# Gated sum of full and sliding-window attention: the sliding branch's weights read with a step of 20, not copied into padded columns

## The chip, the cores and the metric

The kernel runs on one core of a Trainium2 chip. A core has TensorE (matrix products, PE in the profile, with its weight loads as PEld), VectorE (DVE), ScalarE (ACT), GpSimd (POOL) and SyncE (SP, which here only issues DMA transfers), each with its own queue of instructions. The metric is the device time of one execution in microseconds, as the median over the runs.

## What is computed

Two attention branches read the same input x of 2,048 tokens by 640 features, each with its own weights. Both have 32 heads of 20 channels. A gate per token mixes them:

```python
g = _sigmoid((x * gate_w).sum(-1, keepdims=True))
a = _A_ref(x, A_wqkv, A_wo)
b = _B_ref(x, B_wqkv, B_wo)
return g * a + (1 - g) * b
```

Branch A is full softmax attention: `scores = q @ k.T * 20**-0.5` over all 2,048 keys, softmax, times v, then the output projection `wo`. Branch B, the sliding branch, lets each token see eight keys, at distances 0, 2, ... 14 behind it:

```python
off = jnp.arange(W) * dil          # W = 8, dil = 2
idx = pos[:, None] - off[None, :]
mask = idx >= 0
...
logits = jnp.einsum("bhsd,bhswd->bhsw", q, kg) * scale
logits = jnp.where(mask[None, None, :, :], logits, -1e9)
attn = _softmax(logits, axis=-1)
o = jnp.einsum("bhsw,bhswd->bhsd", attn, vg)
```

## The kernel before

**Branch A, the main loop.** The work on scores is cut into 32 groups (a block of 512 queries times four heads), and each group into 64 units (128 keys by 512 queries of one head). The main loop at the end of `_build` takes two or three units as a tile: `qk` (line 1610) writes their scores to PSUM, `exp` (line 1634) lets ScalarE compute the exponentials of the whole tile, and `pv` (line 1679) multiplies them by the values into `obank`. There are 704 tiles. When three units don't fit or the planner chooses so, a further unit "rides" on a tile: VectorE computes its exponential by integer arithmetic on the bits of the number (line 1624 writes `uD`), and three shifted copies of it (line 860 writes `eD`) are weighted and summed by further matmuls against scaled values `vS`, which GpSimd prepares (line 852). A ride thus moves work from ScalarE to VectorE and TensorE.

**Side work.** Between the tiles TensorE runs everything else on three PSUM banks (`side`): A's key, query and value projections (`gen_kd`, `gen_qd`, `gen_v`), the normalisation (`gen_norm`), the output projection (`gen_fold`), the gate, and all of branch B. The helper `mm_group` (line 605) issues these as matmuls in four column groups of 32 output rows; all of them stand at line 620 in the profile. Each has a weight load (LDWEIGHTS) of 128 rows by 32 columns.

**Branch B.** It goes in eight blocks of 256 tokens (`TOK`). `gen_bproj(u)` projects q, k and v of a block: 3 x 5 chunks of 128 output rows, each summed over 5 chunks of features, so 75 steps of four matmuls of 256 columns. VectorE casts the results to `qkvB` (line 919), and SP's queue copies v, shifted, to `vR` (line 927). `gen_b(u)` multiplies q by the shifted k on VectorE (line 945), sums over channels by matmuls with a selection matrix (line 955), takes the maximum and the exponential, multiplies by the shifted v (line 1042), sums (line 1052), and scales (line 1075). Channels are arranged so that chunk f holds channels f, 5 + f, 10 + f and 15 + f of all 32 heads: row 32 j + h of chunk f is channel 5 j + f of head h. Dense weights have that column at 20 h + 5 j + f, so the 32 columns of one weight load lie 20 elements apart.

**How B's weights come into that order.** One transfer (line 1440) brings B's q, k and v weights, dense, into the buffer `stage`. `gen_bweights` (line 869) then copies them on GpSimd in 15 pieces of 128 x 640 (line 878) into the buffer `kvw`, in the padded order, over A's weights: v's part (m = 2) goes over the padded key weights of A's first heads, q's part (m = 0) over A's key weights once A's key projection is done, and k's part (m = 1) over A's value weights once A's last value projection is done. The first `gen_bproj` waits for all of them (`done["bw"]`). `stage` is later used for the products of q and k and for `vR`.

**What sets the order.** Nothing is ordered at run time but by semaphores. A planner in Python (`_Sched`, and `step`, `order`, `run_side`, `next_tile`, `wanted` in `_build`) keeps a modelled clock for each engine, gives each instruction a modelled duration, and from that decides which generator goes next, whether a tile gets two or three units, and whether a unit rides. It has knobs: slack, priorities and idle thresholds. The table `PLAN` (line 50) gives all 18 knobs anew at certain tile numbers; it is the layout table of the change. Where TensorE would idle too long, the planner inserts filler matmuls (line 1700).

Of the kernel before, what the change touches and what calls it, by code (L numbers as in the profile page):

```python
# [6 lines left out]
BF16 = mybir.dt.bfloat16  # L7
# [7 lines left out]
P = 128  # L15
S = 2048
D = 640
H = 32
DH = 20
# [358 lines left out]
def _build(ctx, nc, A_x, A_wqkv, A_wo, B_wqkv, B_wo, gate_w, out):  # L378
# [20 lines left out]
    xT = sb([P, CN, S], BF16, "xT")  # L399
    WqP = sb([P, CN, P], BF16, "WqP")  # L400
    woA_z = _ap(WqP, 0, [[1, D]])
    kvw = sb([P, 3 * CN * D], BF16, "kvw")
    woA_d = sb([P, CN, D], BF16, "woA_d")
    woBp = sb([P, CN, D], BF16, "woBp")
    kT = sb([P, NQ, S], BF16, "kT")
# [1469 lines left out]
```

## Time and profile before

| what | value |
|---|---|
| median of three runs | 815.27 us (813.67 to 817.51) |
| profiled execution, its own time | 818.97 us |
| span of its instructions | 816.4 us |
| granted TensorE clock, mean | 0.991 |
| ScalarE busy | 782.7 us, 96% |
| TensorE busy | 753.3 us, 92% |
| VectorE busy | 718.1 us, 88% |
| GpSimd busy | 149.6 us, 18% |
| weight copies on GpSimd (line 878) | 15, 22.1 us, the first at 72.6 us and the last at 177.8 us |

In a group row, the columns after the bar are busy time in us and mean duration of one instruction in ns, then the idle time of the engine just before them and what ended it; `out<-in` names the buffers. In a timeline row, the first two numbers are start and duration in us, `xN` is the number of instructions merged into the row, and the bracket is the idle time before it. In a window row, each engine has its busy time in us and its count of instructions; PEclk is the clock that TensorE was granted, 1.00 being full speed. Busy times of TensorE are modelled at their ends: matmuls follow each other at a smaller distance than the duration of one.

### The profile page before, as it was taken

To read this page: it belongs to the slowest core of one execution; us is meant where nothing else is said; L and a number is where in the kernel's file an instruction comes from. 1 tells how busy PE (TensorE), PEld (TensorE's weight loads), DVE (VectorE), ACT (ScalarE), POOL (GpSimd) and SP (SyncE) were. 2 spreads that over 40 slices of the span, in tenths; PEclk is the share of its full clock that TensorE was granted. 3 is DMA by queue.
4 is the path that set the end of the run, shared out by engine and by line. 5 is a ranking of instruction groups with operands and counts; after the bars stand their busy time and mean duration, and the time that the engine had idled before them with its cause. 6 is when DMAs were issued, how large, how long until landed. Compare 5 with 4: busy or idle time off the path is not lost.

```text
span 816.4 us, 28733 instructions
## 1 busy us (share of the span) xinstructions
PE 753.3 (92%) x12136; PEld 276.9 (34%) x12138; DVE 718.1 (88%) x1228; ACT 782.7 (96%) x736; POOL 149.6 (18%) x207
## 2 busy tenths in 40 slices
PE   8999999989989999999898988989899999899987
PEld 5332222323333332333333332332243333333324
DVE  7588988579999999989999999898999899988964
ACT  4999999999999999999999999999999999999994
POOL 6014111351112111121112111121101221110110
PEclk9999999999999999999999999999999999999999
DMA  9112212201012231100121000303100130030210
GB/s 313 38 26 47 47 25 43 71 5 29 14 31 52 50 71 27 35 20 6 38 57 38 18 26 19 67 19 77 29 17 14 48 66 14 7 71 28 58 46 35
DMA packets 61458, 35.50 MB, mean 43 GB/s; under 512 B 27220, under 2 KB 60132, under 8 KB 61332
## 3 DMA queue, kind: packets, MB, share of 16 engines
q1 hardware_dynamic: 61044, 33.36, 16.7%
q8 instruction: 96, 1.57, 0.8%
q10 hardware_dynamic: 288, 0.33, 0.1%
q14 instruction: 30, 0.25, 0.1%
HBM read 12.00 MB, written 2.62 MB: 18 GB/s over the span
## 4 chain that ended last, share of the span: by engine, by line
DVE 30%; PE 26%; ACT 25%; issue 12%; SPq 5%; DMA 1%; POOL 0%; POOLq 0%; ACTq 0%; DVEq 0%
ACT ebuf L1634 24%; DVE uD L1624 11%; DVE eD L860 8%; PE score L1610 7%; PE obank L1679 7%; PE side L620 7%; DVE stage L945 3%; SPq L927 3%; PE score L620 2%; SPq L767 2%; DVE stage L1042 2%; DVE qkvB L919 1%; DVE oTt L821 1%; DMA stage<-qkvB 1%; PE score L1325 1%
## 5 line engine op out<-in xcount | busy, mean ns | idle before, releaser
L1634 ACT ACTIVATE ebuf<-score 128x1024 bf16<-128x1024 f32 (+1 forms) x704 | 770.8, 1252 | 13.7 <-PE score L1610 11.9
L1610 PE MATMUL score<-qT,kT 32*128 32x512 bf16 x2048 | 279.4, 386 | 36.0 <-ACT ebuf L1634 20.2
L1624 DVE TENSOR_SCALAR uD<-score 128x512 int16<-128x512 f32 x371 | 244.7, 680 | 24.3 <-PE score L1610 23.6
L860 DVE TENSOR_SCALAR eD<-uD 128x2048 int16<-128x2048 int16 (+1 forms) x279 | 194.8, 719 | 2.3 <-PE obank L1679 1.5
L1679 PE MATMUL obank<-ebuf,vA 128*21 128x512 bf16 x1677 | 156.6, 389 | 4.6 <-ACT ebuf L1634 1.6
L1610 PEld LDWEIGHTS score<-qT,kT 32*128 32x128 bf16 x2048 | 69.6, 91 | 266.0 <-ACT ebuf L1634 178.3
L852 POOL TENSOR_TENSOR vS<-vA,vw 128x252 bf16<-128x252 bf16 x93 | 69.1, 745 | 298.2 <-PE obank L1679 246.6
L620 PE MATMUL side<-xT,kvw 128*32 128x256 bf16 (+2 forms) x2720 | 118.1, 287 | 4.9 <-DVE qkvB L919 2.5
L1679 PE MATMUL obank<-eD,vS 128*21 128x512 bf16 x1113 | 99.2, 384 | 0.0
L620 PEld LDWEIGHTS side<-xT,kvw 128*32 128x32 bf16 (+1 forms) x2720 | 62.0, 96 | 49.9 <-issue 19.6
L1679 PEld LDWEIGHTS obank<-ebuf,vA 128*21 128x21 bf16 x1677 | 36.8, 89 | 87.5 <-issue 56.6
L827 POOL TENSOR_TENSOR rcp<-rcp,gA 128x16 f32<-128x16 f32 x31 | 9.0, 291 | 288.8 <-DVE rcp L825 288.8
L1042 DVE TENSOR_TENSOR stage<-stage,eB 128x2048 bf16<-128x2048 bf16 x40 | 49.7, 1255 | 1.0 <-DMA stage<-qkvB 1.0
L945 DVE TENSOR_TENSOR stage<-qkvB 128x2048 bf16<-128x2048 bf16 x40 | 49.6, 1263 | 0.1
L919 DVE CAST qkvB<-side 128x512 bf16<-128x512 f32 (+1 forms) x72 | 42.0, 592 | 4.3 <-PE side L620 4.1
L1679 PE MATMUL obank<-uD,vA 128*21 128x512 bf16 x371 | 36.9, 388 | 0.0
L1679 PEld LDWEIGHTS obank<-eD,vS 128*21 128x21 bf16 x1113 | 27.7, 92 | 18.8 <-issue 2.6
L833 POOL TENSOR_TENSOR oN<-oTt,rcp 128x512 bf16<-128x512 f32 x31 | 32.6, 1053 | 2.4
L620 PE MATMUL side<-woBp,oB 128*32 128x512 bf16 (+1 forms) x500 | 25.4, 304 | 1.3 <-DVE dst L724 0.5
L821 DVE STREAM_TRANSPOSE oTt<-obank 128x512 f32<-128x512 f32 x32 | 22.7, 708 | 4.5 <-PE obank L1679 4.4
L620 PE MATMUL side<-woA_d,oTd 128*32 128x512 bf16 (+1 forms) x496 | 25.7, 303 | 0.0
L620 PE MATMUL side<-xT,WqP 128*32 128x512 bf16 x320 | 24.3, 385 | 0.6 <-DVE qkvB L657 0.3
(170 smaller groups left out, 519.3 us busy)
## 6 DMA issues: line engine op xcount, KB each, us to landing
stage<-qkvB SPq DMA_DIRECT2D x128, 80.6 KB
WqP<-in_A_wqkv_dram SPq DMA_DIRECT2D x16, 160.0 KB
stage<-in_B_wqkv_dram SPq DMA_DIRECT2D x1, 2400.0 KB
oTd<-oN SPq DMA_DIRECT2D x108, 20.0 KB
qT<-dst SPq DMA_DIRECT2D x104, 20.0 KB
out_dram<-outsb SPq DMA_DIRECT2D x12, 160.0 KB
kvw<-in_A_wqkv_dram SPq DMA_DIRECT2D x2, 800.0 KB
oTd<-in_A_x_dram SPq DMA_DIRECT2D x2, 640.0 KB
```

Of the source, the lines that this page charges most:

```text
L620: ins = e.matmul(o[j:k, :], l(j) if callable(l) else l[:, j:k], r, start=(first and i == 0), stop=(last and i == n - 1), skip_group_check= ...
L821: T("dve", 0.625, lambda e: e.transpose(oTt[:, :], obank[:, :]), reads=["obank"], writes=["oTt"])
L833: T(en, c2, lambda e: e.tensor_tensor(oo, ii, ib, ALU.mult), reads=["rcp", "oTt"], writes=["oN0"])
L852: T("pool", 0.607, lambda e: e.tensor_tensor(vS[:, d % 2, :, :], _ap(vA, (kb * NQ + q) * 4 * DV, [[0, K - 1], [1, 4 * DV]]), _ap(vw, 0, [[ ...
L860: T("dve", 0.065 + 0.1334 * n, lambda e, k=k, sl=sl: e.tensor_scalar(eD[:, sl % NS, 0:512 * n].bitcast(I16), uD[d % 2][:, 0:512 * n].bitca ...
L919: t = TB(dvc(n * TOK), lambda e, o=o, i=i: e.tensor_copy(o, i), reads=[("side", b)], writes=[key])
L945: TB(dvc(CH, 2), lambda e: e.tensor_tensor(o, i0, i1, ALU.mult), reads=["qB", "kB"], writes=[("prod", i)] + (["stage"] if u == 0 else []), ...
L1042: TB(dvc(CH, 2), lambda e: e.tensor_tensor(o, i0, i1, ALU.mult), reads=["eB"] + [("vR", w4) for w4 in range(4)], writes=[("prod", i)], por ...
L1610: ins = e.matmul(o, kT[32 * j:32 * j + 32, q, kb * P:(kb + 1) * P], qT[g % NQT][32 * j:32 * j + 32, :], start=True, stop=True)
L1624: t = T("dve", 0.598, lambda e: e.tensor_scalar(uD[d % 2][:, 512 * i:512 * (i + 1)].bitcast(I16), side[x], UOFF, 0.0, op0=ALU.add, op1=ALU ...
L1634: exps[s] = T("act", actc(512 * n), lambda e: e.activation(ebuf[s % NE][:, 0:512 * n], score[s % 2][:, 0:512 * n], ACTF.Exp, scale=LN2 / S ...
L1679: ins = e.matmul(obank[32 * j:32 * j + DV, :], v, src, start=(kb == 0), stop=(last and k >= len(lst) - 4), skip_group_check=True)
```

## The change

The padded copies are gone. B's dense weights are loaded into a buffer of their own, `wBs`, and stay there for all eight blocks. The weight loads of `gen_bproj` read them in place: 32 columns with a step of 20 elements. The matmuls and their number stay as they are. The space is found by giving `stage` (products and `vR`) the same memory as `kvw`: it is written only when A's projections of k and v no longer need `kvw`. So `gen_bproj(0)` now waits for the end of the key projection instead of the copies, and before its shifted copies of v, and before the first products in `gen_b`, for A's last value projection. `gen_bweights` and its call are removed. The fourth block of x is staged in `wBs` instead of `stage`. The modelled duration of the projection's matmuls is the same as before.

`PLAN` has other rows: 101 changed ones in place of 99.

```diff
 PLAN = {
-    0: ((0.29, 0.69), 0.16, 1.0, 5.5, 0.94, -1.37, 0.17, 9.99, 7.0, 7.54, 0.6, 0.62, 5.69, 5.04, 0.0, 0.65, 2, -3),
...
+    0: ((0.29, 0.69), 0.16, 1.0, 5.5, 0.94, -1.37, 0.17, 9.99, 5.5, 6.98, 0.6, 0.62, 5.69, 5.04, 0.0, 0.62, 2, -1.5),
...
-    kvw = sb([P, 3 * CN * D], BF16, "kvw")
+    CH = WIN * TOK
+    NCH = 3
+    VW = TOK + DIL
+    kvw = sb([P, max(3 * CN * D, NCH * CH + 4 * CN * VW)], BF16, "kvw")
+    stage = kvw
...
-    stage = sb([P, NCH * CH + 4 * CN * VW], BF16, "stage")
+    wBs = sb([P, 3 * D * CN], BF16, "wBs")
...
-    XOFF = [(oTd, 0), (oTd, 4 * D), (oB, 0), (stage, 2 * D * CN)]
+    XOFF = [(oTd, 0), (oTd, 4 * D), (oB, 0), (wBs, 2 * D * CN)]
...
-    def gen_bweights():
-        for m in (2, 0, 1):
...
-                o = _ap(kvw, (m * CN + c) * D, [[P, CN], [32, 4], [1, 32]])
-                i = _ap(stage, c * 3 * D + m * D, [[1, CN], [CN, 4], [DH, 32]])
-                T("pool", 1.352, lambda e, o=o, i=i: e.tensor_copy(o, i), reads=["stage"],
-                  writes=[("WkA", "WvA", ("WkP", 0))[m], ("wBp", m)])
-        done["bw"] = True
...
     def gen_bproj(u):
         t0 = u * TOK
-        while not (done.get("bw") and (u == 0 or done.get(("bl", u - 1)))):
+        while not (done.get(("kd", CN - 1)) and (u == 0 or done.get(("bl", u - 1)))):
             yield ("cond",)
...
-                        kvw[:, (mm_ * CN + c) * D + f * P:(mm_ * CN + c) * D + (f + 1) * P],
+                        lambda j, mm_=mm_, c=c, f=f: _ap(wBs, c * 3 * D + mm_ * D + CN * (j // 32) + f, [[DH, 32]]),
                         xT[:, c, t0:t0 + TOK]) for c in range(CN)]
-                yield from mm_group(b, mms, [("wBp", mm_)] + XT(t0 // 512), mmc(TOK), first=True, per=2)
+                yield from mm_group(b, mms, ["wBs"] + XT(t0 // 512), mmc(TOK), first=True, per=2)
...
-        while u > 0 and not done.get(("bp", u - 1)):
+        while not (done.get(("bp", u - 1)) if u else done.get(("v", KBN - 1, 1))):
...
-              reads=["vB"], writes=[("vR", w4)] + (["stage"] if u == 0 else []), dma=True, nd=4, iss=0.65)
+              reads=["vB"], writes=[("vR", w4)] + (["WkA", "WvA", ("WkP", 0)] if u == 0 else []), dma=True, nd=4, iss=0.65)
...
     def gen_b(u):
-        while not (done.get(("bqk", u)) and (u == 0 or done.get(("bs", u - 1)))):
+        while not (done.get(("bqk", u)) and done.get(("v", KBN - 1, 1)) and (u == 0 or done.get(("bs", u - 1)))):
...
-               reads=["qB", "kB"], writes=[("prod", i)] + (["stage"] if u == 0 else []), port=True)
+               reads=["qB", "kB"], writes=[("prod", i)] + (["WkA", "WvA", ("WkP", 0)] if u == 0 else []), port=True)
...
-    T("sp", 10.0, lambda e: e.dma_start(_ap(stage, 0, [[3 * D, CN], [1, 3 * D]]), wB_v[:, :, :]), writes=["stage", ("xs", 3)], dma=True, iss=2.0)
+    T("sp", 10.0, lambda e: e.dma_start(_ap(wBs, 0, [[3 * D, CN], [1, 3 * D]]), wB_v[:, :, :]), writes=["wBs", ("xs", 3)], dma=True, iss=2.0)
...
-                if g1 == 2:
-                    add_gen(gen_bweights(), 4)
```

More of the change, by code (lines that the diff above doesn't have):

```diff
@@ L443, in _build @@
     vB = _ap(qkvB, CN * TOK + CN * (TOK + PADB), [[TOK + PADB, CN], [1, TOK + PADB]])
-    CH = WIN * TOK
-    NCH = 3
-    VW = TOK + DIL
-    stage = sb([P, NCH * CH + 4 * CN * VW], BF16, "stage")
+    wBs = sb([P, 3 * D * CN], BF16, "wBs")
     vR = _ap(stage, NCH * CH, [[VW, 4 * CN], [1, VW]])
@@ L867, in gen_d @@
         ulock[d % 2] = False
-    def gen_bweights():
-        for m in (2, 0, 1):
-            while m == 0 and not done.get(("kd", CN - 1)) or m == 1 and not done.get(("v", KBN - 1, 1)):
-                yield ("cond",)
-            for c in range(CN):
-                while sch.avail["pool"] > max(sch.avail["pe"], clock[0]):
-                    yield ("cond",)
-                o = _ap(kvw, (m * CN + c) * D, [[P, CN], [32, 4], [1, 32]])
-                i = _ap(stage, c * 3 * D + m * D, [[1, CN], [CN, 4], [DH, 32]])
-                T("pool", 1.352, lambda e, o=o, i=i: e.tensor_copy(o, i), reads=["stage"],
-                  writes=[("WkA", "WvA", ("WkP", 0))[m], ("wBp", m)])
-        done["bw"] = True
     bdone = [0.0]
```

198 rows, old and new, of the table PLAN are left out of this document.

## The prediction

> **What bounds the kernel now.** I read four views in this order: the page, the windows (busy time of each engine by stage), the groups of instructions by shape, and the timeline of single stretches.
>
> ```profile
> span 816.4 us, 28733 instructions
> ...
> PE 753.3 (92%) x12136; PEld 276.9 (34%) x12138; DVE 718.1 (88%) x1228; ACT 782.7 (96%) x736; POOL 149.6 (18%) x207
> ...
> DVE 30%; PE 26%; ACT 25%; issue 12%; SPq 5%; DMA 1%; POOL 0%; POOLq 0%; ACTq 0%; DVEq 0%
> ```
>
> The page names ScalarE: 96% busy. The chain that ended last passes through VectorE, TensorE and ScalarE about equally, and GpSimd (POOL) has 0% of it. So the 22 us of copies that the change removes are worth nothing as GpSimd time; they count only by what they do to others.
>
> ```profile
> core 0: us, PE busy (x) PEld busy (x) DVE busy (x) ACT busy (x) POOL busy (x), PEclk, DMA share, GB/s
> ...
> 140.00:168.00 28.00, 27.18 (x452) 10.37 (x450) 16.82 (x32) 27.00 (x27) 8.54 (x8) 1.00 0.23 57
> 168.00:187.00 19.00, 16.74 (x193) 4.43 (x195) 16.37 (x25) 17.43 (x18) 11.81 (x10) 0.91 0.05 10
> 187.00:300.00 113.00, 106.37 (x1819) 40.73 (x1819) 108.87 (x177) 111.94 (x104) 18.45 (x27) 1.00 0.17 40
> 300.00:500.00 200.00, 184.40 (x3007) 64.71 (x3004) 187.74 (x324) 198.09 (x192) 35.73 (x52) 1.00 0.12 29
> 500.00:700.00 200.00, 183.81 (x3065) 68.14 (x3062) 185.96 (x304) 199.28 (x186) 31.75 (x48) 0.99 0.17 38
> 700.00:800.00 100.00, 92.27 (x1596) 34.91 (x1597) 83.26 (x137) 99.21 (x93) 12.16 (x20) 0.98 0.18 42
> ```
>
> From 187 us on ScalarE is busy within 1% of the time. There only less ScalarE work shortens the kernel, that is, more units ("rides") whose exponential VectorE computes. From 140 to 187 us ScalarE idles 2.6 us and VectorE 13.8 us, while from 140 to 168 us TensorE is full (27.18 of 28).
>
> ```profile
> L1634 ACT ACTIVATE ebuf<-score 128x1024 bf16<-128x1024 f32 x435 | 424.8, 1082 | 10.0 <-PE score L1610 8.3
> L1634 ACT ACTIVATE ebuf<-score 128x1536 bf16<-128x1536 f32 x269 | 382.6, 1526 | 3.7 <-PE score L1610 3.6
> L1624 DVE TENSOR_SCALAR uD<-score 128x512 int16<-128x512 f32 x371 | 244.7, 680 | 24.3 <-PE score L1610 23.6
> L860 DVE TENSOR_SCALAR eD<-uD 128x2048 int16<-128x2048 int16 x276 | 193.4, 721 | 2.3 <-PE obank L1679 1.5
> L620 PE MATMUL side<-xT,kvw 128*32 128x256 bf16 x2400 | 91.8, 274 | 3.3 <-DVE qkvB L919 2.5 <-DVE qbnd L754 0.3
> L620 PEld LDWEIGHTS side<-xT,kvw 128*32 128x32 bf16 x2710 | 62.0, 96 | 49.6 <-issue 19.6 <-DVE qkvB L919 10.8 <-DVE qbnd L754 2.2
> L878 POOL COPY kvw<-stage 128x640 bf16<-128x640 bf16 x15 | 22.1, 1476 | 9.5 <-PE score L620 8.9
> ```
>
> These give the rate of exchange. A unit on ScalarE costs 424.8/(435 x 2) = 0.488 us in a tile of two and 382.6/(269 x 3) = 0.474 us in a tile of three; I use 0.48. A ride costs VectorE 0.680 us plus its share of the shifted copies, 193.4/371 = 0.52 us: 1.20 us. So 1 us of VectorE time that becomes usable is worth 0.40 us of the end.
>
> **The change part by part.**
>
> *Copies gone (line 878).* Fifteen copies of 1,476 ns leave GpSimd. What they do to VectorE stands in the timeline (start, duration; engines mixed; the first row is the group of line 673):
>
> ```profile
> L673 DVE TENSOR_SCALAR KMd<-KMd,kmd 128x32 bf16<-128x32 bf16 x5 | 2.8, 567 | 0.2
> 74.41 0.94 DVE L673 TENSOR_SCALAR KMd<-KMd,kmd 128x32 bf16<-128x32 bf16 x1
> 81.21 1.67 DVE L860 TENSOR_SCALAR eD<-uD 128x2048 int16<-128x2048 int16 x1
> 142.05 1.20 DVE L673 TENSOR_SCALAR KMd<-KMd,kmd 128x32 bf16<-128x32 bf16 x1
> 169.60 1.10 DVE L860 TENSOR_SCALAR eD<-uD 128x2048 int16<-128x2048 int16 x1
> 171.82 0.68 DVE L860 TENSOR_SCALAR eD<-uD 128x2048 int16<-128x2048 int16 x1
> 173.73 4.57 DVE L860 TENSOR_SCALAR eD<-uD 128x2048 int16<-128x2048 int16 x3
> 174.20 5.27 POOL L878 COPY kvw<-stage 128x640 bf16<-128x640 bf16 x3
> 176.59 0.52 PE L1679 MATMUL obank<-ebuf,vA 128*21 128x512 bf16 x4 [0.48 <-DVE eD L860]
> 178.74 0.61 PE L1610 MATMUL score<-qT,kT 32*128 32x512 bf16 x3
> 179.40 1.02 ACT L1634 ACTIVATE ebuf<-score 128x1024 bf16<-128x1024 f32 x1 [1.06 <-PE score L1610]
> 180.88 10.29 ACT L1634 ACTIVATE ebuf<-score 128x1024 bf16<-128x1024 f32 x10 [0.46 <-PE score L1610]
> ```
>
> A shifted copy takes 0.68 us alone (171.82) but three take 4.57 us beside three weight copies: 2.5 us lost there, 1.0 at 81.21, 0.4 at 169.60, and some 1.7 in the two small scalings at 74.41 and 142.05, which without that take (2.8 - 0.94 - 1.20)/3 = 0.2 us each. Together 5.6 us of VectorE, or 5.6 x 0.40 = **2.2 us**. Bounds: 0, if VectorE idles instead, since it isn't full before 168 us, and 2.2. I take 2.2 because 2.9 us of it lie in the stretch where rides are running.
>
> The same three slow copies hold TensorE (0.48 us), after which its matmuls of 0.39 us take 0.52 to 0.61, and the granted clock is 0.91 over 168 to 187 us. ScalarE then waits 1.06 and 0.46 us: **1.5 us** straight on the bounding engine. Bounds 0 (another gap opens at that place) and 1.5; I take 1.5, since the waiting instruction names its releaser.
>
> *Earlier start of the sliding branch.* Its first projection waited for the copies:
>
> ```profile
> 167.95 0.59 PE L620 MATMUL score<-kvw,xT 128*32 128x320 bf16 x12
> 187.09 1.16 PE L620 MATMUL side<-xT,kvw 128*32 128x256 bf16 x36
> ```
>
> The condition is now the end of the key projection alone; the last value projection (167.95 row) gates only the first products, because they now overwrite the dense weights. The branch can start about 19 us sooner. Its work is unchanged, so the gain is VectorE idle time that gets filled: 2.6 us in 168 to 187 us, and little of the 11.2 us in 140 to 168, where TensorE has 0.8 us free for a block's 75 x 0.109 = 8.2 us of projections. 3 us x 0.40 = **1.2 us**; bounds 0 and 13.8 x 0.40 = 5.5. The first value shifts on SP's queue move forward with it; nothing of SP bounds (5% of the chain). The load of the sliding weights keeps its place and size in SP's order. The new waits, on the readers of the dense weights, cost nothing where the value projection is over; if that cover went (products ready before 168 us), VectorE's queue would stand for the difference.
>
> *2,400 weight loads with a step of 20.* These rows show what hides a load now:
>
> ```profile
> 198.87 0.95 PE L620 MATMUL side<-xT,kvw 128*32 128x256 bf16 x28
> 402.81 0.33 PE L1004 MATMUL side<-xT,gwT 128*32 128x64 bf16 x20 [0.18 <-DVE qbnd L754]
> 402.80 0.21 PEld L1004 LDWEIGHTS side<-xT,gwT 128*32 128x32 bf16 x20 [0.52 <-DVE qbnd L754]
> ```
>
> Four column groups run side by side, so 28 matmuls are 7 steps. With 0.274 us for the last, a step is (0.95 - 0.274)/6 = 0.113 us; undisturbed, 256 columns run at 0.109. The 96 ns of a load are a latency: at 402.80 twenty loads of the same width end within 0.21 us, so a step of four occupies at most (0.21 - 0.096)/4 = 29 ns. A step of projection thus hides about 80 ns more. What a step of 20 adds, no row of TensorE shows. The nearest is line 878 itself, which reads with that step: 1,352 ns at its usual length for 640 columns, 2.1 ns a column, 68 ns for 32. Four loads side by side at that price fit under 109 ns. Then only the first load of a burst is exposed: the three quoted bursts of such matmuls (187.09, 198.87, and the row below) hold 36, 28 and 36, mean 33, so 2,400 are some 70 bursts, at most the 360 tasks of the plan. Taking 100 bursts and half of 68 ns: 3.4 us of TensorE, of which 26%, its share of the chain, reaches the end: **0.9 us** lost. Bounds: 0, and 360 x 68 ns = 24 us x 0.26 = 6.4 us.
>
> ```profile
> 597.57 1.17 PE L620 MATMUL side<-xT,kvw 128*32 128x256 bf16 x36
> ```
>
> [...]
>
> *Shared place for dense weights and products, and memory.* The two buffers trade sizes; no instruction is added: 0.
>
> *The layout table.* Nearly all of its rows change, so the order of every tile may. No row prices a table; the nearest are two stretches under the present one:
>
> ```profile
> 300.00:500.00 200.00, 76.36 (x116) 1.00 0.12 29
> 500.00:700.00 200.00, 63.31 (x97) 0.99 0.17 38
> ```
>
> These are the rides (line 1624) by window: 116 against 97 in 200 us, 19 x 0.48 = 9.1 us. I take 0 and keep 9 us on either side.
>
> *Sum.* -2.2 - 1.5 - 1.2 + 0.9 + 0 = -4.0 us. The profiled execution took 818.97 us, 2.6 more than its span and 3.7 more than the median of 815.27; the difference goes onto the median: 811.3, and rounded **811 us**.
>
> **The rivals.**
>
> *The loads set the pace* (slower). It decides once four loads occupy more than 109 ns, 3.4 ns a column side by side, or 0.85 ns a column if the four share one reader. For it: 2.1 ns on GpSimd. Against: the 29 ns of four contiguous loads. At 135 ns a step, 600 steps lose 15.6 us of TensorE; half is covered by its idle 46 us between 187 and 800 us: 811 + 8 = 819. One behind another at 68 ns, a step takes 272 ns: 98 us lost, less cover (46 us idle, as much of filler matmuls again, three quarters usable): about 840. [...]
>
> *The new table is worse* (slower): fewer rides at the rate of 500 to 700 us for 200 us more: 811 + 9 = 820.
>
> *The gain stays off the end* (same): TensorE is full until 168 us and VectorE's regained time turns into idle time; the ScalarE gap reopens. Then 815.3 + 0.9 = 816.
>
> *The table finds more* (faster): VectorE idles 47 us between 187 and 800 us; a third of it ridden is 15.7 x 0.40 = 6.3 us: 805.
>
> **How the numbers follow.** Forecast 0.40 (811, own range 807 to 815), loads at 819: 0.07, at 840: 0.06, worse table 0.14, gain lost 0.16, better table 0.17. About 0.5%, 4.1 us, is what a measurement here can tell from no change, so faster means below 811.2 and slower above 819.3. Faster: 0.17 and 0.26 of the forecast's 0.40, 0.43. Slower: 0.06, half of 0.07, 0.12 of the worse table, and the rest of the tails, 0.26. Same: 0.31. The range 803 to 822 leaves out the 840 case and the ends of both tables, under 0.2.
>
> **What would show it.** Right: no rows of line 878, shifted copies near 0.68 us at 70 to 190 us, a clock near 1.00 at 168 to 187 us, first 256-column projections before 187 us, more than 371 rides, bursts still at 0.109 us a step. Wrong: a step above 0.12 us, loads well over 97 ns with TensorE gaps before score matmuls, or as many rides as before.

## The result, and the profile after

| | before | after |
|---|---|---|
| median of five runs | 817.34 us (813.67 to 817.53) | 809.12 us (807.35 to 810.18) |
| ratio | | 0.9911, 95% interval 0.9885 to 0.9937 |
| profiled execution, its span | 818.97, 816.4 us | 810.18, 808.3 us |
| granted TensorE clock of the profiled execution | 0.991 | 0.996 |
| rides; tiles | 371; 704 | 376; 707 |

The change made the kernel 0.9% faster: 8.2 us between these medians, where 4.0 us were forecast. A second measurement (below) gave 7.3 us.

The page of the changed kernel: busy time of the engines, and the shares of the chain that ended last.

```profile
span 808.3 us, 28593 instructions
...
PE 749.0 (93%) x12063; PEld 285.9 (35%) x12065; DVE 721.9 (89%) x1236; ACT 779.0 (96%) x739; POOL 129.3 (16%) x193
...
PE 34%; DVE 32%; ACT 20%; issue 11%; SPq 1%; DMA 1%; POOL 0%; DVEq 0%; ACTq 0%; POOLq 0%
```

GpSimd lost 20.3 us of work and VectorE gained 3.8. What counts is ScalarE: its work fell from 782.7 to 779.0 us, and its idle time (span less work) from 33.7 to 29.3. So 3.7 us of the shorter span are less work on ScalarE and 4.4 us are less waiting.

The same windows as before the change:

```profile
72.00:140.00 68.00, 65.45 (x866) 19.40 (x854) 59.27 (x107) 67.82 (x67) 9.13 (x15) 1.00 0.21 43
140.00:168.00 28.00, 26.99 (x449) 10.54 (x451) 16.00 (x35) 27.84 (x26) 2.85 (x4) 1.00 0.22 55
168.00:187.00 19.00, 18.34 (x310) 7.65 (x302) 17.71 (x30) 18.89 (x19) 3.46 (x6) 1.00 0.10 21
187.00:300.00 113.00, 101.83 (x1593) 38.17 (x1590) 109.72 (x178) 112.01 (x106) 18.61 (x29) 1.00 0.18 41
300.00:500.00 200.00, 186.17 (x3025) 67.43 (x3029) 191.99 (x326) 198.90 (x193) 32.49 (x49) 0.99 0.13 29
500.00:700.00 200.00, 185.85 (x3106) 73.98 (x3098) 189.52 (x312) 199.37 (x191) 36.41 (x51) 1.00 0.18 41
```

ScalarE's busy time (the fourth of the five) rose by 0.84 us in 140 to 168 and by 1.46 in 168 to 187, where the clock went from 0.91 to 1.00. From 72 to 140, a stretch that the prediction did not quote, it rose by 2.3 us; there the kernel before has this row:

```profile
72.00:140.00 68.00, 63.76 (x800) 18.72 (x794) 59.97 (x103) 65.50 (x63) 15.99 (x19) 0.97 0.20 43
```

These three stretches make 4.6 us, as much as all the waiting that went. The groups of the changed kernel that answer to those shown before (line numbers are each kernel's own: L1624 here is the exponential, L1614 the ride):

```profile
L1624 ACT ACTIVATE ebuf<-score 128x1024 bf16<-128x1024 f32 x449 | 435.9, 1080 | 4.6 <-PE score L1600 3.6
L1624 ACT ACTIVATE ebuf<-score 128x1536 bf16<-128x1536 f32 x258 | 365.5, 1500 | 4.0 <-PE score L1600 3.8
L1614 DVE TENSOR_SCALAR uD<-score 128x512 int16<-128x512 f32 x376 | 247.3, 677 | 12.3 <-PE score L1600 11.9
L623 PE MATMUL side<-xT,wBs 128*32 128x256 bf16 x2400 | 96.5, 282 | 2.3 <-DVE qkvB L909 1.5
L623 PEld LDWEIGHTS side<-xT,wBs 128*32 128x32 bf16 x2400 | 68.1, 142 | 33.1 <-issue 16.3
```

Idle time in front of the exponentials fell from 13.7 to 8.6 us. Rides rose by five; counted by window, the first 300 us hold 126 rides in place of 120. A strided weight load takes 142 ns where a dense one took 96. Its first use, and the burst of matmuls above it, in the timeline:

```profile
166.77 0.53 PEld L623 LDWEIGHTS side<-xT,wBs 128*32 128x32 bf16 x20 [0.23 <-issue]
166.78 0.77 PE L623 MATMUL side<-xT,wBs 128*32 128x256 bf16 x20
```

Branch B starts at 166.8 us in place of 187.1. Twenty matmuls are five steps. In the trace the second step of this burst starts 0.166 us after the first, and each later one 0.109 us after the one before. Over all bursts of at least three steps, the first step takes 0.152 us (0.117 before the change) and the later ones 0.109 in both kernels. So the pace is kept, and only the first load of a burst shows.

### The profile page after: what moved, and what is told of

Its sections match the earlier page's. It is cut to its first block, busy times and chain, and to the rows that moved or that the text cites. A ratio compares the mean times of both kernels' runs of the same rounds, so it can differ in the third digit from the quotient of the medians.

```text
span 808.3 us, 28593 instructions
## 1 busy us (share of the span) xinstructions
PE 749.0 (93%) x12063; PEld 285.9 (35%) x12065; DVE 721.9 (89%) x1236; ACT 779.0 (96%) x739; POOL 129.3 (16%) x193
## 3 DMA queue, kind: packets, MB, share of 16 engines
q8 instruction: 96, 1.57, 0.8%
## 4 chain that ended last, share of the span: by engine, by line
PE 34%; DVE 32%; ACT 20%; issue 11%; SPq 1%; DMA 1%; POOL 0%; DVEq 0%; ACTq 0%; POOLq 0%
ACT ebuf L1624 20%; DVE uD L1614 12%; PE score L1600 10%; DVE eD L863 9%; PE side L623 9%; PE obank L1669 9%; PE score L623 3%; DVE kvw L935 3%; DVE kvw L1032 2%; DVE qkvB L909 2%; SPq L917 1%; PE obank L1690 1%; PE score L1315 1%; PE obank L523 1%; PE side L1042 1%
## 5 line engine op out<-in xcount | busy, mean ns | idle before, releaser
L1624 ACT ACTIVATE ebuf<-score 128x1024 bf16<-128x1024 f32 (+1 forms) x707 | 767.2, 1233 | 8.6 <-PE score L1600 7.4
L1614 DVE TENSOR_SCALAR uD<-score 128x512 int16<-128x512 f32 x376 | 247.3, 677 | 12.3 <-PE score L1600 11.9
L863 DVE TENSOR_SCALAR eD<-uD 128x2048 int16<-128x2048 int16 x282 | 200.2, 731 | 1.7 <-PE obank L1669 0.6
L623 PE MATMUL side<-xT,wBs 128*32 128x256 bf16 x2400 | 96.5, 282 | 2.3 <-DVE qkvB L909 1.5
L623 PEld LDWEIGHTS side<-xT,wBs 128*32 128x32 bf16 x2400 | 68.1, 142 | 33.1 <-issue 16.3
L935 DVE TENSOR_TENSOR kvw<-qkvB 128x2048 bf16<-128x2048 bf16 x40 | 48.6, 1233 | 0.0
L1032 DVE TENSOR_TENSOR kvw<-kvw,eB 128x2048 bf16<-128x2048 bf16 x40 | 47.9, 1213 | 0.5 <-DMA kvw<-qkvB 0.5
L623 PE MATMUL side<-xT,kvw 128*32 128x512 bf16 x310 | 24.3, 382 | 0.9 <-DVE qkvB L660 0.3
```

The source lines that it names most:

```text
L623: ins = e.matmul(o[j:k, :], l(j) if callable(l) else l[:, j:k], r, start=(first and i == 0), stop=(last and i == n - 1), skip_group_check= ...
L863: T("dve", 0.065 + 0.1334 * n, lambda e, k=k, sl=sl: e.tensor_scalar(eD[:, sl % NS, 0:512 * n].bitcast(I16), uD[d % 2][:, 0:512 * n].bitca ...
L935: TB(dvc(CH, 2), lambda e: e.tensor_tensor(o, i0, i1, ALU.mult), reads=["qB", "kB"], writes=[("prod", i)] + (["WkA", "WvA", ("WkP", 0)] if ...
L1032: TB(dvc(CH, 2), lambda e: e.tensor_tensor(o, i0, i1, ALU.mult), reads=["eB"] + [("vR", w4) for w4 in range(4)], writes=[("prod", i)], por ...
L1614: t = T("dve", 0.598, lambda e: e.tensor_scalar(uD[d % 2][:, 512 * i:512 * (i + 1)].bitcast(I16), side[x], UOFF, 0.0, op0=ALU.add, op1=ALU ...
L1624: exps[s] = T("act", actc(512 * n), lambda e: e.activation(ebuf[s % NE][:, 0:512 * n], score[s % 2][:, 0:512 * n], ACTF.Exp, scale=LN2 / S ...
```

## The experiments

The theory at first was the prediction's: copies off VectorE's path, one gap closed, an earlier branch B, loads nearly free. The rivals: the loads cost something that the rest hides; the copies cost nothing; the table did it.

### The changed kernel again

Nothing is edited here: the same kernel is measured a second time.

> The changed kernel itself, on the chip of the runs beside it. Every theory: 0.991 of the time before, about 809 us against 817.

808.49 us against 815.79: ratio 0.9905 (0.9882 to 0.9927). The gain is 7 to 8 us. This run is the base for the variants of the changed kernel.

### The loads, dense

```diff
-                        lambda j, mm_=mm_, c=c, f=f: _ap(wBs, c * 3 * D + mm_ * D + CN * (j // 32) + f, [[DH, 32]]),
+                        lambda j, mm_=mm_, c=c, f=f: _ap(wBs, c * 3 * D + mm_ * D + f * P + j, [[1, 32]]),
```

> The changed kernel in the same order, but each weight load reads 32 neighbouring columns in place of 32 with a step of 20 (the sliding branch then uses wrong columns). Theory (only the first load of a burst is exposed): loads fall from about 140 to 97 ns, the steps stay at 0.109 us, some 90 bursts start 0.04 us sooner, 4 us of TensorE of which a third reaches the end: 1 to 1.5 us faster than the changed kernel, 808. Rival 1 (all of the 4 us lie on the path): 805. Rival 2 (the fillers and the waits on ScalarE hide all of it): the same as the changed kernel, 809.

808.22 us, ratio 0.9896 (0.9875 to 0.9917): 0.27 us below the changed kernel in the medians, 0.7 in the means, and the intervals overlap. The groups of the projection:

```profile
L623 PE MATMUL side<-xT,wBs 128*32 128x256 bf16 x2400 | 92.0, 274 | 2.2 <-DVE qkvB L909 1.5 <-DVE qbnd L757 0.2
L623 PEld LDWEIGHTS side<-xT,wBs 128*32 128x32 bf16 x2400 | 55.2, 96 | 35.5 <-issue 16.3 <-DVE qkvB L909 8.4 <-DVE qbnd L757 1.2
```

TensorE works 4.5 us less on this projection (96.5 with the step of 20). At the end the step of 20 costs at most about 2 us, and nothing that can be told from zero. That removes the rival in which loads set the pace.

### Five steps in one kernel

```diff
+                            if i == 0:
+                                ins = e.matmul(o[j:j + 32, :], l(j, 1), r, **st)
+                            elif i == 1:
+                                ins = e.matmul(o[j:j + 32, :], l(j, 4), r, **st)
...
+                            else:
+                                ins = e.matmul(o[j:j + 32, :], l(j, 40), r, **st)
...
-                    ins = e.matmul(side[b][32 * j:32 * j + 32, TQ:2 * TQ], _ap(gwT, c, [[0, 32]]),
+                    ins = e.matmul(side[b][32 * j:32 * j + 32, TQ:2 * TQ], _ap(wBs, c * 3 * D + j, [[DH, 32]]),
```

> The changed kernel in the same order, with other weight loads in the sliding branch's projection: the five chunks of features load their 32 columns with steps of 1, 4, 8, 20 and 40 elements, each on a line of its own, and the 64-column matmuls of the gate sums load with a step of 20 in place of 0 (neither has the right columns). [...] Theory 2 (cost grows with the step): each longer than the last. And the 64-column steps tell what four such loads occupy: if 29 ns or less, twenty matmuls still take 0.33 us; if 42 ns more than a dense load's, 0.45 us or more.

809.24 us, ratio 0.9895 (0.9826 to 0.9964). The loads of each feature chunk, with steps of 1, 4, 8, 20 and 40 elements in this order (mean ns of one after the busy time):

```profile
L625 PEld LDWEIGHTS side<-xT,wBs 128*32 128x32 bf16 x480 | 12.7, 95 | 21.2 <-DVE qkvB L925 8.5 <-issue 7.7 <-DVE oB L1081 1.1
L627 PEld LDWEIGHTS side<-xT,wBs 128*32 128x32 bf16 x480 | 14.1, 108 | 2.7
L629 PEld LDWEIGHTS side<-xT,wBs 128*32 128x32 bf16 x480 | 17.6, 136 | 6.4 <-issue 5.4
L631 PEld LDWEIGHTS side<-xT,wBs 128*32 128x32 bf16 x480 | 18.4, 142 | 0.7
L633 PEld LDWEIGHTS side<-xT,wBs 128*32 128x32 bf16 x480 | 18.0, 140 | 3.4 <-issue 3.2
```

And the timeline of the same kernel, where such loads stand before matmuls of 64 columns:

```profile
226.23 0.40 PEld L1010 LDWEIGHTS side<-xT,wBs 128*32 128x32 bf16 x20 [0.23 <-ACT eB L999]
```

Of these five steps, those of 8, 20 and 40 elements take 136, 142 and 140 ns, 41 to 47 ns more for 32 columns than a step of 1 (95 ns); a step of 4 costs 13 ns more. So theory 2 falls: from 8 to 40 elements the load hardly changes. Why it levels off there, no run shows. The timeline row shows what four loads occupy when short matmuls don't hide them: twenty loads, of 151 ns as the mean of line 1010, end in 0.40 us, so a step of four takes at most (0.40 - 0.15)/4 = 62 ns. The 29 ns of the prediction belong to loads of one column repeated (a step of 0, as the diff shows), not to contiguous ones. At 62 ns, matmuls of 256 columns with 109 ns a step cover them.

### Copies that move almost nothing, in the order before

```diff
-                T("pool", 1.352, lambda e, o=o, i=i: e.tensor_copy(o, i), reads=["stage"],
+                T("pool", 1.352, lambda e, p=(m * CN + c) * D: e.tensor_copy(kvw[:, p:p + 8], stage[:, 0:8]), reads=["stage"],
...
-                        kvw[:, (mm_ * CN + c) * D + f * P:(mm_ * CN + c) * D + (f + 1) * P],
+                        kvw[:, (min(mm_, 1) * CN + c) * D + f * P:(min(mm_, 1) * CN + c) * D + (f + 1) * P],
```

> The kernel before with every instruction in its old place, but each of the fifteen GpSimd copies moves 8 columns in place of 640, and the projection of v reads the weights of k (so the result isn't the reference's). Theory (the copies cost by slowing VectorE beside them; the planner did not know it): the shifted copies beside them fall from 1.1 to 1.8 us to 0.68 us, the clock stays at 1.00 from 168 to 187 us, and the ScalarE gap of 1.5 us at 178 to 181 us closes; no ride can be added at a fixed order, so 1.5 to 3 us less than before, about 815 us against 817. Rival 1 (the copies are the whole of the gain): 8 us less, 809. Rival 2 (the gain is all of the new order): the same as before, 817.

815.04 us, ratio 0.9993 (0.997 to 1.0017): not distinguishable from before. Yet the stretch looks as forecast, in the window and in the timeline of this kernel:

```profile
168.00:187.00 19.00, 17.15 (x244) 5.35 (x236) 16.73 (x31) 19.00 (x19) 5.65 (x11) 1.00 0.06 14
```

```profile
172.28 2.31 DVE L860 TENSOR_SCALAR eD<-uD 128x2048 int16<-128x2048 int16 x3
```

Three shifted copies took 2.31 us (4.57 before), and ScalarE had no gap from 168 to 187 us: 1.57 us more work there than before. None of it reached the end measurably. At 72 to 140 us ScalarE's busy time was still only 65.91 us, so the idle time there doesn't come from the copies' work.

### The copies put back into the new order

```diff
+    def gen_copies():
+        for m in (2, 0, 1):
...
+                o = _ap(outsb[1], 0, [[P, CN], [32, 4], [1, 32]])
+                i = _ap(wBs, c * 3 * D + m * D, [[1, CN], [CN, 4], [DH, 32]])
...
+                t = _Task(sch.n, "pool", "cmp", lambda e, o=o, i=i: e.tensor_copy(o, i), deps)
...
+                sch.lists["pool"].append(t)
```

The fifteen copies run beside an order that was planned without them.

> The changed kernel with every other instruction in its place, and fifteen copies of the old form put back on GpSimd's queue at the old conditions, into a buffer that nobody reads. Theory: they slow VectorE beside them again, by 3 to 6 us in all, and 1 to 4 us of it reach the end: 810 to 813 against 809. Rival 1 (the copies are the whole of the gain): 817. Rival 2 (all of it is the new order): 809.

815.68 us, ratio 0.9987 (0.9971 to 1.0004): 7.2 us slower than the changed kernel, with the same 376 rides and the same early branch B. That is beyond the 810 to 813 of the theory and next to the 817 of the first rival. Two of its windows, and its group of shifted copies:

```profile
72.00:140.00 68.00, 64.12 (x845) 18.99 (x837) 60.07 (x106) 66.72 (x65) 20.15 (x22) 1.00 0.21 43
168.00:187.00 19.00, 16.31 (x259) 6.65 (x259) 15.68 (x25) 15.81 (x15) 9.14 (x9) 0.91 0.07 16
```

```profile
L863 DVE TENSOR_SCALAR eD<-uD 128x2048 int16<-128x2048 int16 x282 | 204.5, 746 | 1.7 <-PE obank L1690 0.7
```

ScalarE lost 1.10 and 3.08 us in these two windows against the changed kernel. In the second it idles 0.96 us from 168 to 172 us and 1.20 from 176 to 179, at a clock of 1.00, after TensorE waited 1.05 and 1.39 us for VectorE; only then, from 179 us on, is the clock halved (its mean is 0.89 over 176 to 180 us and 0.69 over 180 to 184). Copies that the plan doesn't know cost VectorE 4.3 us on the shifted copies (204.5 against 200.2) and can take the whole gain. A part of the 7.2 us goes with the clock: its mean is 0.9935 here and 0.9965 in the changed kernel, which by the two slopes found below is 0.8 to 1.6 us. The whole is more than the kernel before paid, presumably since its plan had placed rides around the copies; no run shows that. So these two experiments put no single price on the copies: out of the old order they give nothing, put into the new one they take all.

### The edit and the table, each alone

The first kernel is the changed one with the old rows of `PLAN`, the second the old code with the new rows; the first row as an example, for the second kernel:

```diff
-    0: ((0.29, 0.69), 0.16, 1.0, 5.5, 0.94, -1.37, 0.17, 9.99, 7.0, 7.54, 0.6, 0.62, 5.69, 5.04, 0.0, 0.65, 2, -3),
...
+    0: ((0.29, 0.69), 0.16, 1.0, 5.5, 0.94, -1.37, 0.17, 9.99, 5.5, 6.98, 0.6, 0.62, 5.69, 5.04, 0.0, 0.62, 2, -1.5),
...
```

> The changed kernel with the layout table of the kernel before. Theory (table and edit belong together: a table is a list of knobs by tile number, and after the first moved instruction every later decision falls differently): much slower than both, by 20 us or more, with far fewer rides than 371 (the program has 304). Rival (the edit carries the gain and the table is a trimming): 809 to 816.

> The kernel before with the layout table of the changed kernel. Theory: as with the edit alone, 20 us or more slower than both (the program has 340 rides). Rival (the table carries the gain): 809.

The edit under the old table: 866.92 us, ratio 1.0601 (1.0503 to 1.0698), with 304 rides. The new table without the edit: 849.68 us, ratio 1.039 (1.0318 to 1.0462), with 340 rides. Each was run twice. The knobs stand at fixed tile numbers; one moved task shifts all that follows. So the two parts' effects can't be added: neither is worth anything without the other. A table must be searched for each code.

### Other orders of both kernels

Here the code stays and `PLAN` alone is searched anew, in the same way for all three; a row of the second table of before as an example:

```diff
-    45: ((0.26, 0.66), 0.39, 1.0, 2.5, 0.49, -1.34, -0.97, 12.9, 7.0, 8.25, 0.52, 0.47, 4.4, 4.0, 0.0, 0.71, 3, 0.0),
...
+    45: ((0.3, 0.57), 0.28, 1.0, 2.5, 0.55, -1.53, -0.83, 13.46, 6.2, 8.21, 0.47, 0.14, 5.09, 5.0, -0.08, 0.7, 3, 1),
...
```

> The kernel before, with its copies on GpSimd and its padded columns, under another layout table: a search from its own table for a shorter plan changed nearly all of the table's rows; 371 rides and 704 tiles, as before. Theory A (part of the gain is luck of one order: the order before happens to run into stalls that the plan does not see, at 108 to 118 us and beside the copies): a new order of the same work misses some of them, and the two retuned tables scatter by several us between 810 and 818; this one 814. Rival B (the gain belongs to the edit, orders of the same work agree): 815 to 817 for both tables, the copies' gap at 168 to 187 us or wherever the copies now lie stays. Rival C (the old table was merely not searched to its end): both tables reach 809 to 811.

> As before_retuned1, with the table of a second search from another random start (371 rides, 704 tiles). Theory A: not the same time as the first table, 2 to 5 us from it, between 810 and 818. Rival B: within 1 us of the kernel before. Rival C: 809 to 811.

> The changed kernel (weights read in place, step 20) under a third table, found by the same kind of search from its own: 378 rides and 708 tiles in place of 376 and 707. Theory A: an order without the changed kernel's luck, 806 to 814; two rides more are worth 0.96 us by themselves, so 808 if nothing else differs. Rival B: 807 to 809, with the clock at 1.00 over 168 to 187 us and no ScalarE gap above 1 us there. If the order before was the unlucky one and not the order after the lucky one, this kernel stays below 811.

| kernel | median, us | ratio to before | rides |
|---|---|---|---|
| before, first new table | 819.31 | 1.0037 (1.0014 to 1.0059) | 371 |
| before, second new table | 814.61 | 0.9977 (0.9956 to 0.9997) | 371 |
| after, new table | 806.41 | 0.9883 (0.9863 to 0.9904) | 378 |

Orders of the same code differ by up to 4.7 us, as theory A said (the first table lies 1.3 us above its range). Rivals B and C fall: the two tables don't agree, and neither reaches 811. But of the orders that were searched for their code, the slowest of the changed code (809.1) lies 5.5 us below the fastest of the old (814.6), so chance in the orders doesn't make the gain, as far as five orders can tell. The new table for the changed kernel is faster than both kernels of this case.

The second new table shows that copies can be had without a gap. Here they slow the same three shifted copies (timeline), and ScalarE still works through (window):

```profile
171.26 4.59 DVE L897 TENSOR_SCALAR eD<-uD 128x2048 int16<-128x2048 int16 x3
171.73 5.33 POOL L915 COPY kvw<-stage 128x640 bf16<-128x640 bf16 x3
```

```profile
168.00:187.00 19.00, 17.29 (x253) 5.67 (x257) 18.56 (x31) 18.90 (x20) 11.87 (x11) 1.00 0.07 15
```

Slow shifted copies alone don't open the gap. The windows of the kernel before, one us each, show what else was there:

```profile
100.00:104.00 4.00, 2.33 (x28) 0.74 (x28) 3.96 (x8) 4.00 (x4) 0.00 (x0) 1.00 0.41 89
104.00:105.00 1.00, 0.78 (x11) 0.31 (x15) 1.00 (x4) 1.00 (x2) 0.00 (x0) 1.00 0.17 40
105.00:106.00 1.00, 1.00 (x14) 0.33 (x10) 0.47 (x1) 1.00 (x2) 0.92 (x2) 0.53 0.08 21
106.00:107.00 1.00, 1.00 (x13) 0.15 (x6) 0.00 (x0) 0.73 (x1) 1.00 (x2) 0.50 0.16 37
107.00:108.00 1.00, 1.00 (x11) 0.16 (x7) 0.00 (x0) 0.00 (x0) 0.24 (x1) 0.50 0.17 41
108.00:109.00 1.00, 1.00 (x12) 0.28 (x15) 0.94 (x2) 0.94 (x2) 0.00 (x0) 0.77 0.02 4
...
176.00:177.00 1.00, 0.52 (x11) 0.23 (x12) 1.00 (x2) 1.00 (x2) 0.96 (x1) 0.87 0.00 0
177.00:178.00 1.00, 1.00 (x16) 0.37 (x12) 1.00 (x1) 1.00 (x2) 0.94 (x2) 0.50 0.00 0
178.00:179.00 1.00, 1.00 (x11) 0.10 (x3) 0.30 (x1) 0.34 (x1) 1.00 (x1) 0.50 0.00 0
179.00:180.00 1.00, 1.00 (x11) 0.28 (x12) 0.60 (x1) 0.60 (x1) 1.00 (x2) 0.50 0.00 0
180.00:181.00 1.00, 1.00 (x18) 0.22 (x11) 0.21 (x2) 0.54 (x2) 0.04 (x1) 0.93 0.00 0
```

TensorE is busy for 2.33 of 4 us, then its clock is halved (0.50) for some 3.4 us, a matmul of 512 columns takes up to 0.634 us in place of 0.379 (line 1700), and ScalarE runs dry (0.73, 0.00). The gap at 178 us, which I had put down to the copies, has the same clock of 0.50, from about 176.7 to 180.1 us. ScalarE lost 1.33 us at the first place and 1.52 at the second: 2.85 of the 4.6 us by which the three stretches of the result differ.

### Less filling for TensorE

If halved clocks were the cost, fewer filler matmuls must make both kernels slower.

```diff
-                ins = e.matmul(o[32 * j:32 * j + 32, :], w[:, 32 * j:32 * j + 32] if best else w[:, :], xT[:, 0, 0:512], start=bool(best),
+                ins = e.matmul(o[32 * j:32 * j + 32, 0:128], w[:, 32 * j:32 * j + 32] if best else w[:, :], xT[:, 0, 0:128], start=bool(best),
```

> The kernel before with its order unchanged; only the 142 groups of filler matmuls (which compute nothing that is used) are shortened from 512 to 128 columns, so that TensorE does some 142 x 0.16 = 23 us less of work that nobody needs. Theory (the gaps that I put down to the copies are stretches in which the granted clock halves after TensorE has been thinly used, and 0.001 of mean clock costs 0.53 us, the slope over 121 executions of ten kernels): the mean clock falls well below 0.995, and the time is 813.8 + 531 x (1 - clock), so 824 at a clock of 0.98. Rival (the clock only records that TensorE had nothing to do; the gaps have other causes): the clock may fall, but the time stays within 2 us of the kernel before, or drops.

> The changed kernel with its order unchanged and its filler matmuls shortened in the same way. Theory: 807.0 + 531 x (1 - clock), so 818 at a clock of 0.98, with ScalarE idle where the clock halves; if the two kernels fall by about the same clock, they stay some 7 us apart, which is the part of the gain that is not clock. Rival: within 2 us of the changed kernel, 807 to 811, whatever the clock.

| | median, us | ratio to before | mean clock of its executions | expected at that clock |
|---|---|---|---|---|
| before, short fillers | 818.94 | 1.0022 (0.9998 to 1.0045) | 0.9866 | 820.9 |
| after, short fillers | 810.44 | 0.9928 (0.9902 to 0.9955) | 0.9897 | 812.5 |

The clock fell in both (before and after have mean clocks of 0.9950 and 0.9965), and both became slower by some 2 us although TensorE had less to do (1.6 and 1.8 us in the means, each at the edge of what can be told from noise). The direction is the theory's. The size is between it and the rival: some 0.25 us for each 0.001 of clock, where the slope inside each kernel (121 executions; the kernels are nine, as the changed one is counted twice in the expectation's ten) was 0.53. The two kernels stay 8.5 us apart.

The profiled execution of the first kernel also answers for the gap. Its order is that of the kernel before, and the three shifted copies beside three weight copies take 4.57 us again (at 173.50 us), yet the clock stays at 1.00 and ScalarE works through:

```profile
172.00:176.00 4.00, 2.92 (x35) 0.74 (x32) 3.96 (x5) 4.00 (x5) 3.94 (x4) 1.00 0.01 4
176.00:180.00 4.00, 3.63 (x57) 1.17 (x57) 3.83 (x7) 4.00 (x5) 3.79 (x3) 1.00 0.00 0
```

So the copies alone don't open it in their own order either. They may still make it likelier: of the five profiled executions with full-size copies there, three have a halved clock between 176 and 184 us (before, first new table, copies put back), of the seven without them none; the edit and the table alone, whose orders differ most, are left aside. How large their part is stays open.

## Why the prediction was right, and where its sizes were not

The direction and the time (811 forecast; 809.1 and 808.5 measured) are right. The gain is about twice the forecast one. Term by term, against 816.42 and 808.85 us, the means of 49 and 11 executions of the two kernels, that is 7.6 us:

- **Copies gone (2.2) and earlier branch B (1.2).** Both were to appear as rides, 3.4 us less ScalarE work. ScalarE's work fell by 3.7 us; five rides are 2.4 of it, six more stand in the first 300 us, and the tiles of the changed kernel are a little shorter. Right in sum. How it splits between the two is open: no run held branch B back under a table as good. With the order fixed, free VectorE time is worth nothing (0.75 us below before in the medians, not told from zero); what it pays where the plan puts rides there, no run shows by itself.
- **The gap (1.5).** It closed at its place, by 1.46 us here and 1.57 with short copies. Its cause was read too simply: the slow copies were there, but it takes a halved clock after a thin stretch of TensorE as well (0.50 from 176.73 us on, after 2.26 busy us in 3.41), which strikes or not, and at other places in other executions. Copies as slow as before left no gap in another order, nor in another execution of the same order; only copies that the plan doesn't know opened gaps at a clock of 1.00. The step "straight on the bounding engine" counted one such event of one execution as a fixed cost. The clock's share of the gain is 1.5 thousandths between the mean clocks, 0.4 us at 0.25 and 0.8 at 0.53. In the two profiled executions it was more: ScalarE idled 3.4 us beside four halved stretches before 800 us (two are shown) and 1.4 us beside two after the change, some 2 of the 4.4 us of waiting.
- **Loads (0.9 lost).** The mechanism held: pace kept (0.109 us a step), only the first load of a burst exposed (a first step of 0.152 us in place of 0.117). A load's record is 46 ns longer where 34 were assumed, and TensorE works 4.5 us more where 3.4 were; 0.3 to 0.7 us reach the end, not told from zero. The 2.1 ns a column of GpSimd gave 68 ns for four loads side by side, and they took at most 62.
- **The layout table (0, between -9 and 9).** This is the term that was mis-sized. It can't be priced by itself, as the table alone is 3.9% slower and the edit alone 6.0%. What stands where I put 0 is 7.6 - 3.7 - 0.4 to 0.8, about 3 us of ScalarE waiting. In the profiled executions it is some 2 us, mostly in 72 to 168 us (1.0, which is 2.3 less the 1.33 at the halved clock, and 0.8). The row of 72 to 140 us, with its clock of 0.97, was in the view I used and would have shown a gap that a new order could close.

Of the rivals, "the table finds more" (805) is nearest beside the forecast; the further table of the changed kernel reached 806.4. With a clock of 1.00 in both profiled executions, the second new table of before has a span of 809.8 us and the new table of after 804.5: 5.3 us, of which 4.4 are ScalarE work (781.3 and 776.9). So most of the gain that is left at equal clocks is ScalarE work, mainly rides, as the sum had it; a rest of 1 to 3 us of waiting isn't traced to one cause.

## What to carry to other kernels

Where an order is planned ahead, removed work is worth what the plan can put in its place: measure an edit under tables searched for it, several for each side, since one table's luck here was worth 2 to 5 us. A strided weight load beside 256-column matmuls cost almost nothing here (0.3 to 0.7 us of 809, not told from zero), so ask what a load hides behind before copying weights into order. Before a gap on ScalarE is put down to its neighbour, look at the granted clock in windows of one us: a halved clock after a thin stretch of TensorE (0.50 for 3.4 us here) looks like contention.

## What the runs showed of the hardware

- In the kernel with five steps, weight loads of 32 bf16 columns took 95, 108, 136, 142 and 140 ns with steps of 1, 4, 8, 20 and 40 elements; four beside each other occupied at most 62 ns at a step of 20.
- In the trace of the kernel before, the granted clock halved (to 0.50) for 3.413 us at a time, without TensorE having been idle: ahead of the first such stretch it was busy for 2.33 of the 4 us from 100 to 104 us.
- Before 800 us, these stretches start there at 105.05, 176.73, 572.68 and 780.89 us, apart by 21, 116 and 61 times their own length. In the 3.41 us ahead of them TensorE was busy for 0.60, 0.66, 0.68 and 0.61 of the time (modelled), while two stretches with 0.65 and 0.64, at 487.34 and 535.13 us (112 and 126 times 3.413 us after the first), had no halved clock behind them. The changed kernel had halved stretches at 317 and 774 us in one execution, at 212, 318 and 796 in another. What decides whether a halved stretch follows a thin one, no run shows.
- In the second new table of before, TensorE was about as thin in the same 4 us (2.41 us busy) and the clock stayed at 1.00:

```profile
100.00:104.00 4.00, 2.41 (x37) 0.93 (x41) 3.96 (x9) 4.00 (x5) 0.42 (x1) 1.00 0.35 77
```

So a thin stretch is a risk and not a certainty, which may be why 49 executions of the kernel before spread over 8 us (812.7 to 821.0), and the five of the new table of after, with a mean clock of 0.9988, over 0.9 (806.0 to 806.9).
